# A filter beside expert layers: one filter part per slot, a fourth slot per unit, and the first transform moved into the plain stage

## Chip, core and metric

The kernel runs on one core of a Trainium2 chip. The metric is the device time of one execution in microseconds (us); lower is better.

## What is computed

The input `x` has 2048 tokens of 512 numbers. It is normalized (`xn`), and the output is a sum of three terms:

```python
xn = _layernorm(x, axis=-1)
return x + _A_ref(xn, A_w_r, A_w_i) + _B_ref(xn, B_wg, B_w1, B_w2)
```

`_A_ref` is a spectral filter: a two-dimensional real Fourier transform, a product with complex weights, and the inverse transform. `_B_ref` is a mixture of experts in which all 8 experts take part (K = 8 of E = 8), so that it is eight dense two-layer networks, each weighted by a gate per token:

```python
h = _gelu(jnp.einsum("nd,edf->nef", xt, w1))
y = jnp.einsum("nef,efd->ned", h, w2)
out = jnp.einsum("ne,ned->nd", cw, y)
```

Each expert has a hidden width of 1792. Every matmul operand is split into a high and a low part (fp32r), and a product is made of three passes over them.

## The kernel before

The hidden width is cut into chunks of 256, 56 in all over the experts. The first four (`N1 = 4`) are worked in the *plain stage*, two at a time in two passes `q`. A pass goes over four groups `t` of 512 tokens: four first-layer products (`mm1`: `s` for the chunk, `f` for its half, 12 matmuls each), then four second-layer products (`mm2`, 12 matmuls each), whose results VectorE adds to `acc` with the gate as factor. In `mm1` ScalarE applies the gelu and casts the result to the high part of `h`; the low part is a subtraction, on VectorE for `f == 0` and on GpSimd (POOL) for `f == 1`. Weights come into a buffer `raw` and are split by `part1` (first layer) and `part2` (second layer): cast on ScalarE, subtraction on POOL.

After each `mm1` and `mm2` group `tick()` lets a generator, `background()`, issue a bit of other work: normalization of the remaining tokens, logits and gates, the sums and differences of x (`sums`) that the later stage needs and their stores to DRAM (`xs`), and copies of tables (`copies`, one `next(copy)` each). Parts yield a cost; `PACE` is the credit per tick, and `NEXT` ends a tick. In the plain stage the scheduler of the language orders the instructions, with edges where `issue_after` asks for them. There are 64 ticks.

The other 52 chunks are taken in pairs, `N2 = 26`, and each pair in two *units* (`i`), 52 units `u`. A unit multiplies 2x2 blocks by seven products instead of eight (a Strassen-Winograd scheme): `layer1` makes seven products of 12 matmuls from x (`xin` loads `b11`, `b21`, `T1` to `T4`, `b22` into three buffers `xr`) with prepared weights, and `layer2`, interleaved with it, makes the seven products of the unit before and adds each into `acc` (`into`, VectorE). The products go to three PSUM tiles `A`, `B`, `C` of two banks; `layer2` puts two products into one tile one after the other, so the second may not start before the first has been added to `acc`. Weights of the next pair are loaded into the single buffer `raw` and split (`prepare`, ScalarE and POOL). Here the order on each engine is pinned to that of the program (`pin`); DMAs are not pinned.

The filter is worked twice (`filtered(0)`, `filtered(1)`: even and odd frequencies), each as 100 parts `(pe, dve, cost)`: a load of tables, 19 parts of the forward transform (with matmuls), 60 parts without matmuls (butterflies `radix4`, `twiddle`, `multiply` and `combine`), another load, and 19 parts of the inverse transform (with matmuls). Every instruction of them is recorded at line 390 (`op`), every DMA at line 179 (`move`). All wait in the queue `chunks`. A unit has three slots for them, in the steps `n` = 0, 2 and 3 of its seven. In `slot_pe` a slot takes one part with matmuls, or parts without as long as their costs add up to at most 3.2; `slot_dve` issues their VectorE and ScalarE work:

```python
while chunks and not (todo and (chunks[0][0] or spent + chunks[0][2] > 3.2)):
    pe, dve, cost = taken()
```

In `dve` of the forward transform the order is: cast and low part of the product `px` (tile X), copy of the product `py` to `Y`, cast and low part of `u`, two more ScalarE operations on X, then the sum or difference of the halves of the next input `us` (`sgn_op`), then the loads of the next `us` (`part`) and the next table (`table`).

In the first unit there is no second layer to interleave, and `X` and `Z` are both made by matmuls with `a11`; in every other unit ScalarE copies `X` to `Z`.

Of the kernel before, what the change touches and what calls it, by code (L numbers as in the profile page):

```python
# [95 lines left out]
def body(ctx: ExitStack, tc: tile.TileContext, io):  # L96
# [282 lines left out]
    def filtered(p):  # L379
# [38 lines left out]
        for k in range(NB + 3):  # L418
# [10 lines left out]
            def dve(k=k):  # L429
                X = None  # L430
                if 0 <= k - 2 < NB:
                    X = quarters("BC"[k % 2])[:, :, :, :R2].rearrange("p i h (c r) -> p i h c r", c=2)
                    of["X", k - 2] = X
                    px = of["px"].rearrange("p (c r) -> p c r", c=2)
                    op(A.copy, X[:, 0, 0], px)
                    low(X[:, 0], px)
# [9 lines left out]
                if X is not None:  # L446
                    op(A.mul, X[:, 1, :, 0], r32(X[:, 0, :, 1]), -1.0)
                    op(A.copy, X[:, 1, :, 1], r32(X[:, 0, :, 0]))
                if k < NB:
                    u1 = of["us", k]  # L450
                    op(V.tensor_tensor, u1[:, :2], u1[:, :2], u1[:, 2:], op=sgn_op)
                if k + 1 < NB:
# [183 lines left out]
    def mm1(w1, t, s, f):  # L636
# [8 lines left out]
        h = hp.tile([P, 2, TB], F32R, name="h")  # L645
        if f == 0:
            nc.scalar.activation(p1, p1, AF.Gelu_apprx_tanh)
            last_dve[0] = split(h, p1)
        else:
            c = hp.tile([P, TB], F32, name="c", bufs=1)  # L650
            nc.scalar.activation(c, p1, AF.Gelu_apprx_tanh)
            for cs in (slice(0, P), slice(P, TB)) if s else (slice(0, TB),):
                last_pool[0] = split(h[:, :, cs], c[:, cs], nc.gpsimd)
# [81 lines left out]
    def background():  # L735

        n4, n8, s8, s0, s1, sp = ln_rest(4, 4), ln_rest(8, 8), ln_stats(8, 8), sums(0), sums(1), spread()
        for part in (
# [7 lines left out]
            gates((1,)), islice(n8, 1), gap(),  # L746
            islice(n8, 2), gap(), islice(n8, 2), gap(),
            islice(n8, 1), islice(s0, 1), gap(),
            islice(n8, 1), gap(),
            islice(n8, 1), islice(s0, 1), gap(),  # L750
            n8, gap(),
            logits_a((2, 3)), gap(), logits_b((2, 3)), gap(), gates((2, 3)), gap(),
            islice(s0, 1), gap(), islice(s0, 1), gap(), s0, gap(),
# [4 lines left out]
        for cost in s1:  # L758
            next(stores, None)
            yield cost  # L760
            yield NEXT
        for _ in stores:
            yield NEXT
        for _ in range(6):
            next(copy)
            yield NEXT
            yield NEXT

    chunks = deque(filtered(0) + filtered(1))
    todo = []  # L770
# [7 lines left out]
    def slot_pe():  # L778

        spent = 0.0  # L780
        while chunks and not (todo and (chunks[0][0] or spent + chunks[0][2] > 3.2)):
            pe, dve, cost = taken()
            spent += 3.2 if pe else cost
            if pe:
                pe()
            todo.append(dve)
# [6 lines left out]
    bg, step1 = background(), iter(())  # L793
    busy, credit, handed = True, 5.0, False

# [6 lines left out]
    def tick():  # L802
# [4 lines left out]
        while delayed and delayed[0][0] <= 0:  # L807
            delayed.pop(0)[1]()
        if handed:
            with tc.issue_after(last_pool[0]), tc.issue_after(last_act[0]):  # L810
                next(step1, None)
# [73 lines left out]

    ahead = {}

# [3 lines left out]
    def xin(n, i):  # L891
        if (n, i) in ahead:
            return ahead.pop((n, i))
        x = xr.tile([P, 2, 2, TB], F32R, name="xr", bufs=3)
        nc.sync.dma_start(r32(x), xs[n][i])
        return x
# [25 lines left out]
    def layer1(c, i, w, hs, old):  # L922
# [14 lines left out]
        product(X, w["a11"], x, True)  # L937
        Z = bank("A")
        if first:
            product(Z, w["a11"], x, True)  # L940
            ahead["T3", i] = xin("T3", i)
            nc.sync.dma_start(raw, io["wb"][0])
        else:
            copy_of(Z, X)
        yield
# [36 lines left out]

        if first:
            B = bank("B")
            product(B, w["s3"], xin("T3", i), True)
        product(Z, w["s1"], xin("T1", i), False)
# [140 lines left out]
    for q in range(N1 // 2):  # L1127
        more = 2 * q + 2 < N1
        for t in range(NT):
            h = ahead_h  # L1130
            for s in range(2):
                for f in range(len(h) if s == 0 else 0, NFT):
                    h.append(mm1(w1[s], t, s, f))
                    if q == 0 and t == 0 and s == 0:
                        with tc.issue_after(last_act[0]):
                            w2.append(part2(f))
                        delay(4, lambda f=f: load_part(2 + f, 0, f))
                if t == 0 and s == 0 and q:
                    w2.append(part2(1))
                    if more:  # L1140
# [15 lines left out]
            if not more and t + 2 == NT:  # L1156
                for _ in bg:
                    pass
                busy, handed = False, True
                early.close()  # L1160
# [3 lines left out]
                xr = ctx.enter_context(tc.tile_pool(name="xr", bufs=1, reuse_waits="tile"))  # L1164
                ahead = {(n, 0): xin(n, 0) for n in ("b11", "b21", "T2")}
        if more:
            w2 = [part2(0)]
    for b in range(NB - 4, NB):
# [9 lines left out]
    for u in range(2 * N2):  # L1178
# [4 lines left out]
        if u == 1:  # L1183
            ahead.update({(n, 1): xin(n, 1) for n in ("b11", "b21", "T2")})
        if i == 1 and c + 1 < N2:
            raw = load(io["wa"][c + 1])
            step1 = prepare(wq, "u", sums1(raw, False), w1q)
# [23 lines left out]
        for n in range(7):  # L1211
            next(one)
            if u and n in (0, 2) and not end:
                slot_pe()
# [70 lines left out]
```

## Time and profile before

| What | Value |
|---|---|
| Median of 3 runs | 2441.81 us (2431.17 to 2442.25) |
| Profiled execution: time, span | 2437.74 us, 2436.0 us |
| TensorE busy | 2346.9 us (96%) |
| VectorE (DVE) busy | 1841.7 us (76%) |
| ScalarE (ACT) busy | 1105.3 us (45%) |
| GpSimd (POOL) busy | 1350.2 us (55%) |
| Mean granted TensorE clock | 0.989 |

Each number of the trace below comes from this one profiled execution. PE is TensorE's matmuls, PEld its weight loads, SP the engine that issues most DMAs. "L390" is line 390 of the kernel. A group's row has the line, the engine, the operation, the tiles it writes and reads, shapes and a count, then the busy time in us and the mean of one in ns. In the order of time a row begins with start and duration, and a bracket tells how long the engine sat idle before it and what ended that. A row of a stretch `A:B` has its length, then per engine the busy time and the number of instructions, the granted clock (1.00 is full), the share of the DMA engines, and GB/s.

The plain stage runs to 225.42 us, where the first matmul of line 880 (the units' products) starts; the units fill the rest.

### The profile page before, as it was taken

To read this page: it belongs to the slowest core of one execution; us is meant where nothing else is said; L and a number is where in the kernel's file an instruction comes from. 1 tells how busy PE (TensorE), PEld (TensorE's weight loads), DVE (VectorE), ACT (ScalarE), POOL (GpSimd) and SP (SyncE) were. 2 spreads that over 40 slices of the span, in tenths; PEclk is the share of its full clock that TensorE was granted. 3 is DMA by queue.
4 is the path that set the end of the run, shared out by engine and by line. 5 is a ranking of instruction groups with operands and counts; after the bars stand their busy time and mean duration, and the time that the engine had idled before them with its cause. 6 is when DMAs were issued, how large, how long until landed. Compare 5 with 4: busy or idle time off the path is not lost.

```text
span 2436.0 us, 28116 instructions
## 1 busy us (share of the span) xinstructions
PE 2346.9 (96%) x10640; PEld 1921.4 (79%) x10640; DVE 1841.7 (76%) x1729; ACT 1105.3 (45%) x1549; POOL 1350.2 (55%) x788
## 2 busy tenths in 40 slices
PE   9998899999988989999999999999999999999999
PEld 7776788887766777888888888777777888888888
DVE  7511577779999999777777777899989777777776
ACT  6422464554433444444445554444444444444441
POOL 2215455565654666555555555765666555566663
PEclk9999999999999999999999999999999999999999
DMA  4772777665655657787766766666656778886663
GB/s 175 268 286 88 257 267 277 245 256 216 234 215 216 220 204 275 268 285 269 255 243 249 249 242 237 216 221 219 229 202 222 284 260 286 286 287 222 238 223 115
DMA packets 130152, 579.13 MB, mean 238 GB/s; under 512 B 13761, under 2 KB 24513, under 8 KB 75105
## 3 DMA queue, kind: packets, MB, share of 16 engines
q1 hardware_dynamic: 129360, 564.65, 64.4%
q10 hardware_dynamic: 656, 12.67, 1.3%
q8 instruction: 85, 1.39, 0.2%
q14 instruction: 51, 0.41, 0.1%
HBM read 541.49 MB, written 48.37 MB: 242 GB/s over the span
## 4 chain that ended last, share of the span: by engine, by line
PE 74%; DVE 19%; issue 3%; DMA 2%; POOL 2%; ACT 1%; SPq 0%; DVEq 0%; POOLq 0%; ACTq 0%
PE B L880 28%; PE C L880 19%; PE A L880 17%; DVE Y L390 5%; PE psf L390 4%; DVE acc L909 3%; DVE c L912 3%; DVE c L932 3%; PE p L642 2%; PE p L667 2%; DVE hs L919 1%; DVE B L390 1%; DVE A L390 1%; DMA raw<-in_wp 1%; DVE c L909 1%
## 5 line engine op out<-in xcount | busy, mean ns | idle before, releaser
L919 POOL TENSOR_TENSOR hs<-c,hs 128x1024 fp32r<-128x1024 f32 x155 | 409.2, 2640 | 404.0 <-ACT hs L916 399.6
L880 PE MATMUL C<-hs,vs 128*128 128x512 f32 x1836 | 452.1, 395 | 16.1 <-DVE acc L909 14.9
L916 ACT CAST hs<-c 128x1024 fp32r<-128x1024 f32 x361 | 379.2, 1051 | 178.2 <-PE B L880 91.7
L880 PE MATMUL B<-xr,ua 128*128 128x512 f32 x1872 | 455.2, 392 | 2.4 <-DVE c L909 1.3
L880 PE MATMUL A<-xr,us 128*128 128x512 f32 x1872 | 454.8, 392 | 1.2 <-issue 1.2
L880 PEld LDWEIGHTS C<-hs,vs 128*128 128x128 f32 x1836 | 345.6, 190 | 95.7 <-DVE acc L909 18.3
L880 PEld LDWEIGHTS B<-xr,ua 128*128 128x128 f32 x1872 | 351.4, 188 | 82.0 <-DVE c L909 3.1
L880 PEld LDWEIGHTS A<-xr,us 128*128 128x128 f32 x1872 | 349.7, 188 | 77.5 <-issue 1.6
L880 PE MATMUL B<-hs,va 128*128 128x512 f32 x1224 | 302.6, 396 | 17.8 <-DVE acc L909 17.8
L912 DVE TENSOR_TENSOR c<-c 128x1024 f32<-128x1024 f32 x204 | 309.1, 1515 | 0.1
L919 DVE TENSOR_TENSOR hs<-c,hs 128x1024 fp32r<-128x1024 f32 x206 | 297.1, 1462 | 1.2 <-ACT hs L916 1.2
L880 PEld LDWEIGHTS B<-hs,va 128*128 128x128 f32 x1224 | 228.9, 189 | 74.0 <-DVE acc L909 24.9
L909 DVE TENSOR_TENSOR acc<-C,acc 128x1024 f32<-128x1024 f32 x198 | 241.3, 1219 | 59.4 <-PE C L880 58.5
L903 ACT ACTIVATE c<-c 128x1024 f32<-128x1024 f32 x104 | 110.4, 1062 | 280.4 <-DVE c L909 280.4
L899 ACT COPY c<-A 128x1024 f32<-128x1024 f32 x104 | 105.6, 1015 | 258.9 <-PE A L880 147.8
L932 DVE TENSOR_TENSOR c<-c,cwb 128x1024 f32<-128x1024 f32 x104 | 162.2, 1560 | 57.5 <-ACT c L903 57.5
L909 DVE TENSOR_TENSOR acc<-B,acc 128x1024 f32<-128x1024 f32 x100 | 122.1, 1221 | 86.8 <-PE B L880 86.7
L621 POOL TENSOR_TENSOR ua<-raw,ua 128x512 fp32r<-128x512 f32 x78 | 118.0, 1513 | 119.7 <-ACT ua L620 119.7
L880 PE MATMUL C<-hs,va 128*128 128x512 f32 x612 | 156.0, 405 | 24.0 <-DVE acc L909 24.0
L909 DVE TENSOR_TENSOR c<-B,c 128x1024 f32<-128x1024 f32 x104 | 127.0, 1222 | 53.1 <-PE B L880 34.2
L880 PE MATMUL B<-xr,us 128*128 128x512 f32 x624 | 152.9, 394 | 10.1 <-DMA xr<-xs_T 10.1
L880 PEld LDWEIGHTS C<-hs,va 128*128 128x128 f32 x612 | 117.2, 194 | 56.3 <-DVE acc L909 30.6
(184 smaller groups left out, 3137.0 us busy)
## 6 DMA issues: line engine op xcount, KB each, us to landing
xr<-xs_T SPq DMA_DIRECT2D x208, 1024.0 KB, 5.7
xr<-xs_b SPq DMA_DIRECT2D x156, 1024.0 KB, 5.3
cwb<-cwd SPq DMA_DIRECT2D x120, 256.0 KB, 5.5
raw<-in_wa SPq DMA_DIRECT2D x26, 1024.0 KB, 4.9
raw<-in_wb SPq DMA_DIRECT2D x26, 1024.0 KB, 4.8
xs_T<-Y SPq DMA_DIRECT2D x8, 1024.0 KB, 6.5
us<-xfd SPq DMA_DIRECT2D x32, 256.0 KB, 3.1
D<-mbd SPq DMA_DIRECT2D x32, 256.0 KB, 3.9
```

The costliest lines, as they stand in the source:

```text
L390: return pin(fn(*args, **kw))
L621: return pin((eng or nc.vector).tensor_tensor(dst[:, 1], src, r32(dst[:, 0]), op=ALU.subtract)).ins
L642: last = nc.tensor.matmul(p1, w1[k][:, hw, f * P : (f + 1) * P], x, start=(n == 0), stop=(n == 11))
L667: last = nc.tensor.matmul(p2, h[f][:, hh, js], w2[f][:, hw], start=(n == 0), stop=(n == 6 * NFT - 1))
L880: pin(nc.tensor.matmul(pt[:, m, :], w[:, hw, k, m * P : (m + 1) * P], x[:, hx, k, :], start=(start and n == 0), stop=(n == 5), skip_group_ ...
L899: last_act[0] = pin(nc.scalar.copy(dst, src)).ins
L903: last_act[0] = pin(nc.scalar.activation(v, v, AF.Gelu_apprx_tanh)).ins
L909: pin(nc.vector.tensor_add(dst, a, b))
L912: pin(nc.vector.tensor_sub(dst, a, b))
L916: main_act[0] = pin(nc.scalar.copy(hs[n][:, 0], src)).ins
L919: op = (nc.gpsimd if pool else nc.vector).tensor_tensor(hs[n][:, 1], src, r32(hs[n][:, 0]), op=ALU.subtract)
L932: pin(nc.vector.tensor_mul(dst, src, g))
```

## The change

- A slot takes exactly one filter part. A fourth slot is opened in step `n == 5` where the next part has matmuls or a cost under 1.3. The three short table loads that follow other parts are merged into the part ahead of them.
- The first 20 parts (the first filter's load and forward transform) are issued by `background()` in the plain stage, one per tick, in place of six copies; five copies move to earlier ticks and the rest are taken in the units.
- `handed` has three values now: the plain stage's last group drains the background only until the x sums are stored, and from then on all h splits are VectorE's.
- In the forward transform the sum or difference of the halves of `us` comes first in `dve`.
- In the second plain pass the second-layer weights are split behind the first `mm1` groups, not ahead of them.
- In the first unit `Z` is copied from `X` as elsewhere; the product with `T3` comes second, into `C`; `b11`, `T3`, `b21` are loaded ahead, and the load of the next first-layer weights is issued behind the second unit's `b11`.

```diff
             def dve(k=k):
                 X = None
+                if k < NB:
+                    u1 = of["us", k]
+                    op(V.tensor_tensor, u1[:, :2], u1[:, :2], u1[:, 2:], op=sgn_op)
...
-                if k < NB:
-                    u1 = of["us", k]
-                    op(V.tensor_tensor, u1[:, :2], u1[:, :2], u1[:, 2:], op=sgn_op)
...
-        if f == 0:
+        if f == 0 or handed > 0:
             nc.scalar.activation(p1, p1, AF.Gelu_apprx_tanh)
             last_dve[0] = split(h, p1)
...
         for _ in stores:
+            part_of_filter()
             yield NEXT
-        for _ in range(6):
-            next(copy)
+        handed = 0
+        while len(chunks) > 177:
+            part_of_filter()
             yield NEXT
-            yield NEXT
-
-    chunks = deque(filtered(0) + filtered(1))
+
+    chunks = deque()
+    for pe, dve, cost in filtered(0) + filtered(1):
+        if chunks and cost < 0.5:
+            ahead_pe, ahead_dve, ahead_cost = chunks.pop()
+            chunks.append((ahead_pe, lambda a=ahead_dve, b=dve: (a(), b()), ahead_cost))
+        else:
+            chunks.append((pe, dve, cost))
+
+    def part_of_filter():
+
+        pe, dve, cost = chunks.popleft()
+        if pe:
+            pe()
+        dve()
...
     def slot_pe():
 
-        spent = 0.0
-        while chunks and not (todo and (chunks[0][0] or spent + chunks[0][2] > 3.2)):
+        if chunks:
             pe, dve, cost = taken()
-            spent += 3.2 if pe else cost
             if pe:
                 pe()
             todo.append(dve)
...
         Z = bank("A")
+        copy_of(Z, X)
         if first:
-            product(Z, w["a11"], x, True)
-            ahead["T3", i] = xin("T3", i)
+            B = bank("C")
+            product(B, w["s3"], xin("T3", i), True)
             nc.sync.dma_start(raw, io["wb"][0])
-        else:
-            copy_of(Z, X)
...
-        if first:
-            B = bank("B")
-            product(B, w["s3"], xin("T3", i), True)
         product(Z, w["s1"], xin("T1", i), False)
...
                     h.append(mm1(w1[s], t, s, f))
+                    if q and t == 0 and s == 1 and f == 0:
+                        w2.append(part2(1))
...
                 if t == 0 and s == 0 and q:
-                    w2.append(part2(1))
+                    w2.append(part2(0))
...
             if not more and t + 2 == NT:
-                for _ in bg:
-                    pass
-                busy, handed = False, True
+                while handed < 0:
+                    next(bg)
+                handed = 1
...
-                ahead = {(n, 0): xin(n, 0) for n in ("b11", "b21", "T2")}
+                ahead = {(n, 0): xin(n, 0) for n in ("b11", "T3", "b21")}
         if more:
-            w2 = [part2(0)]
+            w2 = []
...
         if u == 1:
-            ahead.update({(n, 1): xin(n, 1) for n in ("b11", "b21", "T2")})
+            ahead.update({(n, 1): xin(n, 1) for n in ("b11",)})
+            behind = last_x[0]
+            ahead.update({(n, 1): xin(n, 1) for n in ("b21", "T2")})
         if i == 1 and c + 1 < N2:
-            raw = load(io["wa"][c + 1])
+            with tc.issue_after(behind) if u == 1 else nullcontext():
+                raw = load(io["wa"][c + 1])
...
-            if u and n in (0, 2) and not end:
+            if u and not end and (n in (0, 2) or n == 5 and chunks and (chunks[0][0] or chunks[0][2] < 1.3)):
                 slot_pe()
```

More of the change, by code (lines that the diff above doesn't have):

```diff
@@ L735, in background @@
     def background():
+        nonlocal handed
         n4, n8, s8, s0, s1, sp = ln_rest(4, 4), ln_rest(8, 8), ln_stats(8, 8), sums(0), sums(1), spread()
@@ L746, in background @@
             gates((1,)), islice(n8, 1), gap(),
-            islice(n8, 2), gap(), islice(n8, 2), gap(),
+            islice(n8, 2), gap(), islice(n8, 2), copied(), gap(),
             islice(n8, 1), islice(s0, 1), gap(),
-            islice(n8, 1), gap(),
+            islice(n8, 1), copied(), gap(),
             islice(n8, 1), islice(s0, 1), gap(),
-            n8, gap(),
-            logits_a((2, 3)), gap(), logits_b((2, 3)), gap(), gates((2, 3)), gap(),
+            n8, copied(), gap(),
+            logits_a((2, 3)), gap(), logits_b((2, 3)), copied(), gap(), gates((2, 3)), copied(), gap(),
             islice(s0, 1), gap(), islice(s0, 1), gap(), s0, gap(),
@@ L793, in body @@
     bg, step1 = background(), iter(())
-    busy, credit, handed = True, 5.0, False
+    busy, credit, handed = True, 5.0, -1
     delayed = []
@@ L808, in tick @@
             delayed.pop(0)[1]()
-        if handed:
+        if handed > 0:
             with tc.issue_after(last_pool[0]), tc.issue_after(last_act[0]):
@@ L884, in product @@
                     n += 1
-    ahead = {}
+    ahead, last_x = {}, [None]
     def bank(name):
@@ L894, in xin @@
         x = xr.tile([P, 2, 2, TB], F32R, name="xr", bufs=3)
-        nc.sync.dma_start(r32(x), xs[n][i])
+        last_x[0] = nc.sync.dma_start(r32(x), xs[n][i]).ins
         return x
```

## The prediction

> **What bounds the kernel now.** The page comes first: TensorE (PE) is busy for nearly the whole span, so only its gaps, and work it does twice, are worth time. The waits of PE, summed by releaser, say what its gaps are.
>
> ```profile
> span 2436.0 us, 28116 instructions
> PE 2346.9 (96%) x10640; PEld 1921.4 (79%) x10640; DVE 1841.7 (76%) x1729; ACT 1105.3 (45%) x1549; POOL 1350.2 (55%) x788
> PE C L880 <- DVE acc L909: 38.9, 21, 4.2
> PE B L880 <- DVE acc L909: 17.8, 16, 3.7
> PE B L880 <- DMA xr<-xs_T: 10.1, 1, 10.1
> PE p L642 <- ACT c L651: 5.6, 1, 5.6
> PE p L667 <- POOL h L621: 4.2, 2, 3.0
> ```
>
> Read as: line of the waiting matmul, what released it, total, times, longest. 56.7 us go to matmuls of the second layer that may not write a PSUM bank until VectorE (DVE) has added the last product in it to `acc`. The other three waits are single events near the start.
>
> The waits on DVE lie in two stretches. The next rows give PE's busy time and matmul count there for line 880 alone, for all engines (PE, PEld, DVE, ACT, POOL; granted clock; DMA), and for the filter's line 390 alone; the third stretch has no filter work.
>
> ```profile
> 555.00:945.00 390.00, 355.69 (x1491) 284.01 (x1490) 0.97 0.60 220
> 1490.00:1905.00 415.00, 391.86 (x1664) 313.52 (x1663) 0.99 0.63 224
> 2160.00:2360.00 200.00, 200.00 (x874) 163.61 (x873) 1.00 0.65 233
> ...
> 555.00:945.00 390.00, 355.69 (x1491) 284.01 (x1490) 367.13 (x307) 165.32 (x221) 233.19 (x125) 0.97 0.60 220
> ...
> 555.00:945.00 390.00, 0.00 (x0) 0.00 (x0) 130.87 (x120) 7.90 (x36) 0.97 0.60 220
> 1490.00:1905.00 415.00, 0.88 (x6) 0.86 (x6) 113.13 (x93) 9.17 (x39) 0.99 0.63 224
> ```
>
> Calm matmuls take 200.00/874 = 0.2288 us, so a unit of 168 takes 38.4 us. At that rate the first stretch's 1491 need 341.2 us and the second's 1664 need 380.8 (and 0.9 of the filter's): lost are 48.8 and 33.3, together **82.1 us**. That is more than the waits, because the clock drops after some. These stretches are the filter's steps without matmuls (butterflies, twiddles, multiplication by the weights), two or three in each of three slots per unit. DVE is 94% busy in the first: it is the bound there. Take from the filter's DVE time what a unit absorbs free of loss: (130.87 - 48.8)/8.875 units = 9.25 us in the first, (113.13 - 33.3)/9.9 = 8.06 in the second, 8.6 over both.
>
> **The change, part by part.**
>
> *One part per slot, a fourth slot.* I laid the 177 remaining parts on the 50 units by the new rule (three slots, a fourth where the next part has matmuls or is estimated under 1.3); they end in unit 50. What matters is the DVE time per unit.
>
> ```profile
> 690.00:804.00 114.00, 0.00 (x0) 0.00 (x0) 44.51 (x64) 0.00 (x0) 0.96 0.61 226
> 1638.00:1742.00 104.00, 0.00 (x0) 0.00 (x0) 34.92 (x32) 0.00 (x0) 0.98 0.63 225
> L390 DVE TENSOR_TENSOR Y<-Y 128x1024 f32<-128x1024 f32 x24 | 50.0, 2082 | 0.6
> L390 DVE TENSOR_TENSOR Y<-A,B 128x512 f32<-128x512 f32 x24 | 32.6, 1415 | 0.0
> L390 DVE TENSOR_TENSOR Y<-A,B 128x520 f32<-128x520 f32 x8 | 13.9, 1793 | 0.0
> ```
>
> The first two rows are line 390 while the eight multiply-and-combine pairs run: 5.56 us a pair in the first filter, 4.37 in the second. A butterfly part is one operation of 2.1 us, or at its end two of 32.6/24 = 1.36 (first filter 13.9/8 = 1.74). A butterfly unit then holds 6 to 7 us, under 8.6: no loss. A unit of four multiply parts holds two pairs: 11.1 in the first filter (three units, 2.5 over each), and 6.95 + 5.56 = 12.5 in the unit that two heavy butterfly steps open (3.9 over); in the second, 8.7 three times (0.1 over) and 5.4 + 4.4 = 9.8 once (1.2 over). Remaining loss 13 us; with 9.25 absorbed 9.5, with 8.06 18. Gain: 82.1 - 13 = **69** (64 to 72.6).
>
> By the Trainium skill ("TensorE: Matmul & The Clock Gate", Part 1: the HAM clock gate) the clock is halved only after an idle window of about 3.4 us, so remaining waits of 1 to 3 us would cost no clock. Scaling the 13 by 56.7/82.1 gives 9, and the sum would be 4 lower. I keep the row: 0.97 in a stretch whose longest wait was 4.2.
>
> *First unit.* A second product of `a11` with `b11` becomes a copy by ScalarE, `T3` is fetched ahead instead of `T2`, and the load of the next weights goes behind an x load.
>
> ```profile
> 228.28 2.88 PE L880 MATMUL A<-xr,ua 128*128 128x512 f32 x12
> 231.00 2.88 PE L880 MATMUL B<-xr,ua 128*128 128x512 f32 x12
> 246.74 4.34 PE L880 MATMUL B<-xr,us 128*128 128x512 f32 x12 [10.15 <-DMA xr<-xs_T]
> ...
> 239.24 0.33 SPq L127 DMA_DIRECT2D raw<-in_wa  x1
> 239.67 0.85 SPq L895 DMA_DIRECT2D xr<-xs_T  x2
> ...
> xr<-xs_T SPq DMA_DIRECT2D x208, 1024.0 KB, 5.7
> L899 ACT COPY A<-B 128x1024 f32<-128x1024 f32 x51 | 50.9, 997 | 78.8 <-PE B L880 45.2 <-DVE acc L909 33.6
> ```
>
> The duplicate costs 231.00 - 228.28 = 2.7. The wait of 10.15, with 4.34 - 2.88 = 1.5 of slow clock behind it, exists because SP stood at the weights' load until their buffer was read out (239.24), and the x loads came behind it. All three go: 14.3. Late next are the x loads themselves: three buffers, each free when its product ends, two products (5.5 us) ahead of use, against 5.7 to land and 0.3 to issue; four loads at up to 0.6 put back 2 (0 to 6 if they land 1 us later). The copy of 1.0 lies beside the next two products, and its result is needed after them. The weights' load, some 10 us later, serves unit 2. Net **12.3**.
>
> *Plain stage, stalls.* Second-layer weight casts move behind the gelus, and the last group's h splits go to DVE.
>
> ```profile
> 135.05 1.14 ACT L620 CAST w<-raw 128x512 fp32r<-128x512 f32 x2 [16.81 <-DMA raw<-in_wp]
> 135.75 2.50 POOL L621 TENSOR_TENSOR w<-raw,w 128x512 fp32r<-128x512 f32 x2 [15.72 <-ACT w L620]
> 137.24 7.30 PE L642 MATMUL p<-x,w 128*128 128x512 f32 x24 [5.58 <-ACT c L651]
> 212.70 11.87 PE L667 MATMUL p<-w,h 128*128 128x512 f32 x38 [3.04 <-POOL h L621]
> ```
>
> ScalarE stood 16.81 us at the cast for a late DMA with the gelus behind it: 5.58, and 7.30 - 24 x 0.2288 = 1.8 of slow clock. POOL's h split stood behind the layer weights: 3.04, and 11.87 - 38 x 0.2288 = 3.2. Both go: **13.6**. The casts are late next; from the second one until its product stand one matmul group and half of the next, 4.1 us, against two casts of 0.6 and two POOL subtractions of 1.3: nothing, if the DMA is in. The six queued copies of tables move from 110-170 us to some 48-80 us (the sixth later), where the DMA has room (0.41, below); their price is nothing as long as the x sums there are not on PE's path.
>
> *The first forward transform in the plain stage.* Its PE work (192 matmuls) only moves. New is the pace: one part in each group of 12 matmuls, 12 x 0.2288 + 2 x 0.72 = 4.2 us (0.72 from the next rows: 305.61 - 304.89). In units 2 to 7 a part had 10 us or more. With the sign step first on DVE and two `us` buffers, a part's load starts only after the low part of the one before: 3.1 to land, 0.3 to issue, three DVE steps of 0.42 make 4.7.
>
> ```profile
> 304.89 0.88 PE L390 MATMUL psf<-A,uz 128*128 128x260 f32 x6
> 305.61 0.62 PE L880 MATMUL C<-hs,vs 128*128 128x512 f32 x2
> us<-xfd SPq DMA_DIRECT2D x32, 256.0 KB, 3.1
> L390 DVE TENSOR_TENSOR uz<-us,uz x16: 409/425/1418, 287.2 to 500.0; 128x256 fp32r<-128x256 f32 x16
> ...
> 40.00:80.00 40.00, 39.67 (x194) 30.09 (x193) 25.09 (x65) 20.61 (x35) 2.71 (x3) 1.00 0.41 132
> 120.00:160.00 40.00, 34.42 (x144) 27.64 (x143) 7.47 (x10) 7.99 (x16) 7.74 (x8) 0.91 1.01 399
> 160.00:200.00 40.00, 40.00 (x178) 33.03 (x177) 8.98 (x13) 8.85 (x17) 5.44 (x6) 1.00 0.23 84
> ...
> q10 hardware_dynamic: 192, 5.25, 22.3%
> A<-f0d SPq DMA_DIRECT2D x1, 520.0 KB, 21.0
> 137.24 10.20 SPq L179 DMA_DIRECT2D us<-xfd  x2
> ```
>
> 16 parts x (4.7 - 4.2) put back **8** (0 to the bounds below). By the Trainium skill ("DMA: Bandwidth & Descriptors", Anatomy of one DMA, measured on another queue kind) 256 KB would take 2.0 + 0.6 us, the loop would keep pace and the sum would be 8 lower; the landing of 3.1 decides. The parts start at some 112 us, by my count of the ticks, in a DMA that is full until about 160 (1.01) with loads landing in up to 21.0. The copies that leave were 5.25 of that part's traffic (22.3%), but the filter's loads come in. Behind a waiting load stands DVE, and behind it the evictions of PE's banks. One first landing of 21 against three banks' room (8.2 us) and the two parts before the first matmul (8.4): 4, twice over for table and input: **8**. Queued on SP behind these loads are the next raw weights, needed 50 us later, and stores. DVE and ScalarE have room (7 to 9 of 40 us).
>
> Sum, against the profiled execution's 2437.74 us (span 2436.0 and 1.7 around it; 4.1 under the shown median 2441.81): 2437.7 - 69 - 12.3 - 13.6 + 8 + 8 = **2359**.
>
> **The rivals.** *A, the transform is paced by a full DMA.* If its first six parts wait as the second `us` load did (10.2 us behind the first, row above), they cost 6 x (10.2 - 4.2) = 36 instead of 8: 2387. For it: 1.01 at 120-160 us; against: 0.23 right after, and the copies gone.
>
> *B, the fourth slot hurts locally.* It puts a part ahead of the sixth and the next unit's first step, where DVE has most of its own work.
>
> ```profile
> 695.98 3.02 PE L880 MATMUL C<-hs,vs 128*128 128x512 f32 x12 [1.39 <-DVE acc L909]
> ```
>
> There a part at the first slot already made the eviction late by 1.39. 29 units have four parts; at 1.3 each: 2359 + 38 = 2397. Against: 8.6 us absorbed per unit, and matmul parts lengthen PE's own work.
>
> *C, slower.* If every one of the 16 steps in the plain stage waits for a landing of L, each costs L + 1.6 - 4.2. The other terms gain 95, so this decides from L = 8.5 us; at 10 us throughout it costs 118, and the time is 2461. For it: landings of 10 to 21 in the full stretch; against: the median of 3.1, and that most steps fall after 140 us.
>
> *D, nothing gained,* if the waits on DVE return in full inside units: its total work stays. Against: over the span DVE is busy 76%.
>
> **How the numbers follow.** Chances: forecast 0.66, A 0.12, B 0.12, C 0.06, D or mixtures near no change 0.04. The forecast's own range is 2337 (72.6 + 14.3 + 13.6 gained, nothing put back) to 2378. Up to B's 2397 the range leaves out C and D. Faster by over 0.5% 0.90, within 0.5% 0.04, slower 0.06; 0.5% (12 us) is about what a measurement of this kernel can tell from no change.
>
> **What would show it.** Right: waits of PE on `acc` fall from 56.7 to about 10, in the first filter's multiply units; the filter's line 390 shows matmuls from about 120 us; no PE wait on `xr` over 2 us; the waits on `c` and `h` in the plain stage gone. Wrong: PE waits at `psf` or on DVE between 110 and 190 us (A, C), or at `C` and `B` once per unit all along (B).

## The result, and the profile after

The changed kernel takes 2372.85 us (2369.38 to 2374.64, four runs) against 2441.72 before: a ratio of 0.9726 [0.9697, 0.9755]. The forecast was 2359, with a range of 2337 to 2397. The profiled execution took 2369.38, against 2437.74 before: 68.4 us less, where the sum of the terms had promised 79.

Two lines of the page after, and the waits of TensorE by releaser (line, what released it, total, times, longest). Line 880 is now 894, 909 is 923, 899 is 913.

```profile
span 2367.6 us, 28129 instructions
PE 2328.6 (98%) x10628; PEld 1909.1 (81%) x10628; DVE 1897.2 (80%) x1731; ACT 1107.9 (47%) x1549; POOL 1373.9 (58%) x785
```

```profile
PE C L894 <- DVE acc L923: 6.2, 4, 2.3
PE B L894 <- DVE c L923: 4.8, 6, 1.5
PE B L894 <- ACT A L913: 3.7, 1, 3.7
PE B L894 <- DVE acc L923: 3.5, 8, 0.8
PE A L894 <- issue: 2.4, 2, 1.2
```

The 56.7 us on `acc` have become 6.2 + 3.5 = 9.7, the wait on `xr` near the start is gone, and of those on `c` and `h` there 0.6 and 0.2 are left. VectorE is busy 55.5 us longer (1897.2 against 1841.7) for the same arithmetic and two h splits more.

The same parts now lie elsewhere, so the stretches differ: the first two rows hold the filter's steps without matmuls, the third the worst of them. Columns: length, PE and PEld busy time with counts of the products alone, granted clock, DMA share, GB/s.

```profile
320.00:980.00 660.00, 648.04 (x2802) 525.19 (x2801) 1.00 0.68 245
1380.00:2050.00 670.00, 667.15 (x2898) 542.82 (x2897) 1.00 0.66 236
530.00:700.00 170.00, 161.04 (x686) 128.55 (x685) 0.99 0.64 235
```

At 0.2288 us a matmul the first loses 660 - 641.1 - 0.9 (six filter matmuls) = 18.0, the second 670 - 663.1 = 6.9: **24.9** where 82.1 were lost before, so 57.2 gained. The forecast left 13. The 170 us around the first filter's multiplication lose 170 - 157.0 = 13.0 of it; the other 11.9 are scattered, 5.0 in the rest of the first stretch and 6.9 in the second.

The units start at 244.60 us (225.42 before). At start to start (0.72 for six) the 192 matmuls moved ahead of them are 23.0 us, so the plain stage lost 23.0 - 19.2 = 3.8 less than it did. The first unit, from its first product to the one behind the first two of the second layer, before and after, in order of time:

```profile
225.42 3.02 PE L880 MATMUL B<-xr,ua 128*128 128x512 f32 x12 [0.84 <-DVE acc L671]
...
269.10 2.92 PE L880 MATMUL B<-xr,ua 128*128 128x512 f32 x12
```

```profile
244.60 2.98 PE L894 MATMUL B<-xr,ua 128*128 128x512 f32 x12 [0.94 <-DVE acc L671]
...
282.18 2.91 PE L894 MATMUL B<-xr,ua 128*128 128x512 f32 x12
```

43.7 us became 37.6: 6.1 gained. Together 57.2 + 3.8 + 6.1 = 67.1 of the 68.4; 1.3 lie outside these places.

### The profile page after: what moved, and what is told of

The parts are those of the page before. It is cut to its first block, busy times and chain, and to the rows that moved or that the text cites. A ratio compares the mean times of both kernels' runs of the same rounds, so it can differ in the third digit from the quotient of the medians.

```text
span 2367.6 us, 28129 instructions
## 1 busy us (share of the span) xinstructions
PE 2328.6 (98%) x10628; PEld 1909.1 (81%) x10628; DVE 1897.2 (80%) x1731; ACT 1107.9 (47%) x1549; POOL 1373.9 (58%) x785
## 4 chain that ended last, share of the span: by engine, by line
PE 80%; DVE 14%; DMA 2%; ACT 1%; issue 1%; POOL 1%; SPq 0%; ACTq 0%; POOLq 0%; DVEq 0%
PE B L894 30%; PE C L894 20%; PE A L894 20%; PE psf L390 4%; PE p L642 3%; DVE Y L390 3%; PE p L667 2%; DVE c L946 2%; DVE acc L923 2%; DVE c L926 2%; DVE c L923 1%; DVE hs L933 1%; DVE B L390 1%; ACT c L917 1%; DVE A L390 1%
## 5 line engine op out<-in xcount | busy, mean ns | idle before, releaser
L933 POOL TENSOR_TENSOR hs<-c,hs 128x1024 fp32r<-128x1024 f32 x155 | 415.5, 2681 | 330.1 <-ACT hs L930 325.9
L933 DVE TENSOR_TENSOR hs<-c,hs 128x1024 fp32r<-128x1024 f32 x206 | 311.7, 1533 | 1.2 <-ACT hs L930 1.2
L926 DVE TENSOR_TENSOR c<-c 128x1024 f32<-128x1024 f32 x204 | 297.8, 1460 | 0.0
L923 DVE TENSOR_TENSOR acc<-C,acc 128x1024 f32<-128x1024 f32 x198 | 241.1, 1218 | 58.2 <-PE C L894 57.7
L894 PEld LDWEIGHTS B<-hs,va 128*128 128x128 f32 x1224 | 228.3, 188 | 56.7 <-DVE acc L923 6.9
L946 DVE TENSOR_TENSOR c<-c,cwb 128x1024 f32<-128x1024 f32 x104 | 177.9, 1711 | 57.5 <-ACT c L917 57.5
L621 POOL TENSOR_TENSOR ua<-raw,ua 128x512 fp32r<-128x512 f32 x78 | 132.4, 1697 | 143.6 <-ACT ua L620 143.6
L923 DVE TENSOR_TENSOR acc<-B,acc 128x1024 f32<-128x1024 f32 x100 | 122.1, 1221 | 61.5 <-PE B L894 61.1
L621 POOL TENSOR_TENSOR va<-raw,va 128x512 fp32r<-128x512 f32 x78 | 138.2, 1772 | 45.6 <-ACT va L620 44.2
L894 PE MATMUL C<-hs,va 128*128 128x512 f32 x612 | 149.6, 393 | 1.5 <-DVE acc L923 1.5
L894 PE MATMUL A<-hs,vs 128*128 128x512 f32 x612 | 148.6, 391 | 0.0
```

Source lines behind the costliest of these rows:

```text
L621: return pin((eng or nc.vector).tensor_tensor(dst[:, 1], src, r32(dst[:, 0]), op=ALU.subtract)).ins
L894: pin(nc.tensor.matmul(pt[:, m, :], w[:, hw, k, m * P : (m + 1) * P], x[:, hx, k, :], start=(start and n == 0), stop=(n == 5), skip_group_ ...
L923: pin(nc.vector.tensor_add(dst, a, b))
L926: pin(nc.vector.tensor_sub(dst, a, b))
L933: op = (nc.gpsimd if pool else nc.vector).tensor_tensor(hs[n][:, 1], src, r32(hs[n][:, 0]), op=ALU.subtract)
L946: pin(nc.vector.tensor_mul(dst, src, g))
```

## The experiments

Times are medians. Each set of kernels was timed beside its own runs of the kernel before, whose median was 2435.75 to 2441.72; ratios to it are given where a few us matter. The changed kernel itself ran again only beside two of them, the product and the sign step last; the others are compared with its 2372.85, and its own two medians differ by 3.5.

**The old slots.** Does the spreading bring the gain (theory S) or the move of the transform (theory M)?

```diff
-        if chunks:
+        spent = 0.0
+        while chunks and not (todo and (chunks[0][0] or spent + chunks[0][2] > 3.2)):
             pe, dve, cost = taken()
+            spent += 3.2 if pe else cost
...
-            if u and not end and (n in (0, 2) or n == 5 and chunks and (chunks[0][0] or chunks[0][2] < 1.3)):
+            if u and n in (0, 2) and not end:
```

> The changed kernel with the old slot rule: three slots per unit, parts without matmuls taken together up to an estimate of 3.2; the first forward transform stays in the plain stage. Theory S (spreading: a unit takes in some 8.6 us of filter work on VectorE, more makes TensorE wait): the two stretches without filter matmuls lose some 80 us again instead of 25, so 2373 + 57 = 2430 us, with 50 to 60 us of TensorE waits on acc. Rival M (the gain comes from the first transform's move, which leaves VectorE more room in all): the gain stays, 2373 to 2385 us.

2417.95, ratio 0.9918 [0.9892, 0.9945]; the waits on `acc` are back (line numbers differ by two):

```profile
PE C L896 <- DVE acc L925: 35.1, 17, 4.2
PE B L896 <- DVE acc L925: 11.2, 7, 2.5
```

S holds, 12 us under its 2430: spreading alone is worth 45 us. It isn't the whole 57 of the stretches. From the units' start to the end this kernel takes 2415.9 - 245.03 = 2170.9, the changed one 2123.0: 47.9 for spreading. The kernel before takes 2210.6, of which 23.0 are the moved matmuls and 6.1 the first unit, so 2181.5. By this subtraction the last 10.6 go with the 20 parts that no longer have to be placed in units; no run shows them by themselves.

**The transform back in the units**, with the fourth slot open to every part.

```diff
         for _ in stores:
-            part_of_filter()
             yield NEXT
         handed = 0
-        while len(chunks) > 177:
-            part_of_filter()
-            yield NEXT
...
-            if u and not end and (n in (0, 2) or n == 5 and chunks and (chunks[0][0] or chunks[0][2] < 1.3)):
+            if u and not end and n in (0, 2, 5):
```

> The changed kernel with the first forward transform back in the units, one part per slot, and the fourth slot open to every part (197 parts in 200 slots). Theory S: the 23 us of matmuls only go from the plain stage to the units, and the butterflies now stand four to a unit (8 to 9.5 us on VectorE, just over what a unit takes in), so the loss in the stretches grows from 25 to 35-50 us: 2383 to 2400 us. Rival M: without the move the gain is lost, 2425 us or more. Rival P (the move costs, because the plain stage waits for loads): 2365 us or less.

2387.30, ratio 0.9785 [0.976, 0.981], in theory S's range: the move is worth 14.5. The units start 25.4 us earlier (219.20), with 23.0 us of matmuls less ahead of them: beyond its own matmuls the transform costs the plain stage 2.4, where the forecast put back 16. From the units' start to the end this kernel needs 2384.2 - 219.20 = 2165.0, of which 23.0 are those matmuls: 19.0 more than the changed kernel. So the gain of the move is the room it leaves in the units (under a slot rule that differs in the fourth slot); there the waits rise:

```profile
PE C L890 <- DVE acc L919: 12.0, 6, 2.3
PE B L890 <- DVE c L919: 7.4, 9, 1.1
PE B L890 <- DVE acc L919: 6.0, 7, 1.1
```

**GpSimd without reads.** Left out of the computation here: the low parts of the units' weights and of their layer inputs that GpSimd makes; it writes zeros there instead. Theory L says that what still is lost comes from VectorE operations that last longer beside GpSimd's.

```diff
-                split(to[n], src.rearrange("p (k f) -> p k f", k=2), nc.gpsimd)
+                main_act[0] = pin(nc.scalar.copy(to[n][:, 0], src.rearrange("p (k f) -> p k f", k=2))).ins
+                pin(nc.gpsimd.memset(r32(to[n][:, 1]), 0.0))
...
-        op = (nc.gpsimd if pool else nc.vector).tensor_tensor(hs[n][:, 1], src, r32(hs[n][:, 0]), op=ALU.subtract)
+        op = nc.gpsimd.memset(r32(hs[n][:, 1]), 0.0) if pool else nc.vector.tensor_tensor(hs[n][:, 1], src, r32(hs[n][:, 0]), op=ALU.subtract)
```

> The changed kernel, in which GpSimd writes zeros in place of the low parts of the layer inputs and weights that it makes in the units (those low parts are left out of the computation); it reads no SBUF for them and is shorter. Theory L (a VectorE operation with two SBUF inputs is held up while GpSimd reads SBUF, and this makes the remaining loss of 25 us): VectorE's twiddle step falls from a median of 1.5 to 0.42 us, its 128x1024 operations to some 1.22, VectorE's busy time by 150 us or more, the loss to under 8: 2350 to 2358 us. Rival W (the parts are just too much work per unit, whatever GpSimd does): durations within 5% and 2368 to 2375 us.

2345.95, ratio 0.9613 [0.9584, 0.9642]. The same VectorE work takes 1642.3 us instead of 1897.2, and no wait on `acc` is left in the list. Groups of VectorE in the changed kernel, then here (count, busy time in us, mean in ns):

```profile
L390 DVE SCALAR_TENSOR_TENSOR Y<-Y,C 128x256 f32<-128x256 f32 x27 | 30.6, 1169 | 0.0
L390 DVE TENSOR_TENSOR us<-us 128x256 f32<-128x256 f32 x32 | 27.1, 848 | 10.0 <-DMA us<-xfd 10.0
```

```profile
L390 DVE SCALAR_TENSOR_TENSOR Y<-Y,C 128x256 f32<-128x256 f32 x27 | 10.3, 419 | 0.0
L390 DVE TENSOR_TENSOR us<-us 128x256 f32<-128x256 f32 x32 | 14.8, 463 | 12.5 <-DMA us<-xfd 12.5
320.00:980.00 660.00, 658.19 (x2869) 538.19 (x2868) 1.00 0.70 252
1380.00:2050.00 670.00, 670.00 (x2922) 548.23 (x2921) 1.00 0.67 239
```

The two stretches lose 660 - 656.4 - 18 x 0.12 (filter matmuls) = 1.4, and 670 - 668.6 = 1.4: of the 24.9 some 22 are gone. Theory L holds. The total passes its range by 4: from the units' start at 252.83 to the end it is 28.5 us less in all, and 5.5 of that are the first unit (284.87 - 252.83 = 32.0 instead of 37.6), whose copy no longer waits.

GpSimd's work is shorter here too (693.3 us busy instead of 1373.9), and some of its reads remain, so the trace can tell reading from mere work. VectorE's `c<-c,cwb`, both inputs in SBUF, keeps its 1.23 us at 582.03, while GpSimd writes zeros from 582.45 to 582.98. `B<-Y,D` takes 1.79 us at 573.37, beside a GpSimd operation that reads `raw` from 572.89 to 574.61, and 0.69 at 591.73, beside no GpSimd instruction.

**The first unit's copy on VectorE.** In the changed kernel a wait that the forecast didn't have stands there: `X` to `Z`, ScalarE's copy. First PE, then ScalarE, in order of time:

```profile
247.42 2.88 PE L894 MATMUL C<-xr,us 128*128 128x512 f32 x12
253.99 4.59 PE L894 MATMUL B<-xr,ua 128*128 128x512 f32 x12 [3.69 <-ACT A L913]
...
250.85 0.62 ACT L620 CAST vs<-raw 128x512 fp32r<-128x512 f32 x1 [2.90 <-POOL raw L852]
...
252.94 1.00 ACT L913 COPY A<-B 128x1024 f32<-128x1024 f32 x1
```

The copy stands in ScalarE's queue behind four weight casts, the first of which waits 2.90 us for GpSimd.

```diff
-        copy_of(Z, X)
+        if first:
+            pin(nc.vector.tensor_copy(Z, X))
+        else:
+            copy_of(Z, X)
```

> The changed kernel with the first unit's copy of X to Z on VectorE instead of ScalarE. Theory Q (the copy stands behind weight casts in ScalarE's queue, which wait for GpSimd): TensorE's wait of 3.7 us there goes, and 1.7 of slow clock behind it: 2373 - 5 = 2368 us. Rival X (the first unit is paced by its x loads and PSUM copies anyway): the wait comes back one or two products later, 2371 to 2374 us.

2367.89, ratio 0.9708 [0.9687, 0.9729]. The wait on the copy is gone, a wait of 1.27 on `xr` is next, and from the units' start to the product used above the kernel needs 281.08 - 249.03 = 32.1 us instead of 37.6. Theory Q holds in the trace: 5.5 gained there. The medians show 2 to 5 of it; the profiled execution shows 1.6 (2367.75 against 2369.38), because its units start 4.4 us later.

**The product instead of the copy.** As before the change, but with the x loads and `T3`'s product in the new order.

```diff
-        copy_of(Z, X)
+        if first:
+            product(Z, w["a11"], x, True)
+        else:
+            copy_of(Z, X)
```

> The changed kernel with the first unit's second accumulator made by the product once more, as in the kernel before, instead of the copy from PSUM to PSUM; the x loads stay in their new order. Theory Q (the copy is late in ScalarE's queue, and the step itself is what cost the first unit its gain): the product costs 2.7, and the waits of 3.7 on the copy and of 1.2 and 1.15 on the accumulator's reading go: 2368 to 2371, 2 to 5 us less than the changed kernel beside it. Theory X (behind the copy stands the fetch of x, which would be late by as much): a wait on xr of 3 us or more takes its place, and the time is 2373 to 2380.

2369.38, ratio 0.9730 [0.9711, 0.9749], beside 2369.37 of the changed kernel. The time lies in theory Q's range, but not its 2 to 5 us less: the totals are the same. In the trace the stretch takes 284.59 - 248.97 = 35.6, 2.0 less, with a wait of only 0.92 on `xr`, so X falls; but the plain stage ended 4.4 later. So in the first unit of these two executions the copy on ScalarE costs 2 more than the product it replaced. The new order, of the loads and of `T3`'s product together, brought 43.7 - 35.6 = 8.1.

**A fifth slot.** If the first filter's multiply units are too full (S), they should be spread further.

```diff
-            if u and not end and (n in (0, 2) or n == 5 and chunks and (chunks[0][0] or chunks[0][2] < 1.3)):
+            if u and not end and (n in (0, 2) or n in (4, 5) and chunks and (chunks[0][0] or n == 5 and chunks[0][2] < 1.1)):
```

> The changed kernel with one more place per unit that may take a filter part with matmuls (after the unit's fifth vector operation), while a small part without matmuls may stand only at the last place. Theory S (what is left of the loss in the first filter's multiply units is the same cause as before: parts whose matmuls cover less than their vector work, now 8 parts of the two heavy units that stand too close): more spreading takes 6 to 10 us off the 24.8 us that the two stretches still lose, 2363 to 2367 against 2372.9. Theory L alone (vector operations that stand beside GpSimd's are the whole remainder, and spreading can't help them, only put more of them beside GpSimd): 2370 to 2376, with the wait of product on acc not smaller than 6.2 + 3.5 us.

2367.94, ratio 0.9711 [0.9685, 0.9737]. The 170 us of the multiplication, and the waits:

```profile
530.00:700.00 170.00, 166.03 (x720) 134.43 (x720) 1.00 0.70 253
```

```profile
PE B L894 <- DVE acc L923: 8.4, 11, 1.6
PE B L894 <- DVE c L923: 2.2, 4, 0.6
```

720 matmuls: 5.3 lost instead of 13.0. The same parts need not lie in the same 170 us here, but the two whole stretches agree: 2840 and 2900 matmuls, 10.2 + 6.5 = 16.7 lost instead of 24.9. The wait at `C` is gone from the list, that at `B` grew from 3.5 to 8.4. The 8.2 are in theory S's 6 to 10, and the 8.4 on `acc` are less than L alone allows (6.2 + 3.5). The total, between the two theories' ranges, shows 1 to 5 of them against the two medians of the changed kernel.

**The best of both**: the fifth slot and the copy on VectorE (both edits above).

> The changed kernel with the five places and the first unit's copy from PSUM to PSUM on VectorE. If the two act in different places they add: the copy gave 5.0 us (2367.9), the fifth place 6 to 10 by theory S, so 2358 to 2362; by theory L alone no better than 2366 to 2370.

2361.84 (2361.53 to 2364.26), ratio 0.9689 [0.9664, 0.9715]. It lies in the range forecast and under all nine runs of the changed kernel (2368.65 to 2374.64). From the units' start to the end the trace has 2359.8 - 246.10 = 2113.7, so 9.3 less than the changed kernel; the copy alone has 6.0 less, the fifth slot alone 4.7. The two nearly add, as acts in different places should.

**The old cast order** in the second plain pass.

```diff
-                    if q and t == 0 and s == 1 and f == 0:
-                        w2.append(part2(1))
...
-                    w2.append(part2(0))
+                    w2.append(part2(1))
...
-            w2 = []
+            w2 = [part2(0)]
```

> The changed kernel with the plain stage's weight casts in the order that the kernel before had. Theory P (the reordering is what took the waits on c and h of 5.58 + 1.8 us out of the plain stage): 2378 to 2381, with a wait of the first groups' or the plain stage's matmuls on ScalarE of 4 to 7 us. Theory F (the first transform's matmuls, which now stand in the plain stage, fill those waits whatever the order is): 2371 to 2375, and no such wait over 2 us.

2371.42, ratio 0.9725 [0.9694, 0.9756], and the wait on `c` is 0.6 us in all. The time is F's. But the edit doesn't bring the old order back: in the plain stage the scheduler orders the instructions, and ScalarE, VectorE and GpSimd have the same sequence of rows in this trace as in the changed kernel's. So neither theory is tested, and what the order is worth stays open. The rows of the weights' load and its cast, in order of time, of the kernel before, of this one and of the changed kernel:

```profile
118.67 5.86 SPq L135 DMA_DIRECT2D raw<-in_wp  x2
```

```profile
136.84 1.20 SPq L135 DMA_DIRECT2D raw<-in_wp  x1
149.77 0.62 ACT L620 CAST w<-raw 128x512 fp32r<-128x512 f32 x1
```

```profile
136.64 1.18 SPq L135 DMA_DIRECT2D raw<-in_wp  x1
149.56 0.62 ACT L620 CAST w<-raw 128x512 fp32r<-128x512 f32 x1
```

In the last two the load is issued 18 us later and the cast doesn't wait at all, where ScalarE stood 16.81 us before. Whether that comes from the copies that left this stretch or from the groups that now stand ahead wasn't tried apart.

**The last h splits on GpSimd again.**

```diff
-        if f == 0 or handed > 0:
+        if f == 0:
```

> The changed kernel with the last plain group's splits of h on GpSimd again, as in the kernel before, not on the engines that the change chose. If they set the plain stage's end (theory H): the wait of 3.04 + 3.2 us at the last groups returns, 2376 to 2379, and the units start 3 to 6 us later after the last plain group's matmuls. If the other work of the stage covers them (theory F): 2371 to 2375.

2377.60, ratio 0.9745 [0.9717, 0.9773]. The wait of 3.04 of the kernel before returns:

```profile
242.11 8.91 PE L667 MATMUL p<-w,h 128*128 128x512 f32 x38 [3.03 <-POOL h L621]
```

The slow clock behind it doesn't: 38 matmuls take 8.91 us, and took 11.87 before. So this edit is worth 3, not 6.2 (4.8 by the medians; the runs overlap). The units of this execution start 7.3 later, at 251.86, but 2.6 of that stand before the filter's first matmul (152.79 against 150.22), ahead of the edit.

**The changed kernel once more, and the sign step last.**

> The changed kernel once more, unaltered, beside the next two. 2369 to 2376 us. What it is to tell is how far the end of the plain stage moves from execution to execution of the same instructions: kernels whose plain stage is the same as here started their units at 244.6, 246.1, 248.5, 249.0 and 252.8 us. Theory V (it is no property of the kernels but varies by run): a start of the units other than 244.6, by 1 to 8 us, with the same instructions. Theory K (each kernel has its own): 244.6 within 0.5.

> The changed kernel with the forward transform's sign step after the other vector steps of its part, as in the kernel before, not ahead of them. Theory N (its place is nothing, since a part's load has time enough): within 2 us of the changed kernel beside it. Theory P (in the plain stage a part's load is the pace, and the sign step first lengthens the way from one landing to the next load, as my prediction had it with 0.5 us a part): 4 to 8 us less than the changed kernel beside it, the units starting that much earlier.

```diff
-                if k < NB:
-                    u1 = of["us", k]
-                    op(V.tensor_tensor, u1[:, :2], u1[:, :2], u1[:, 2:], op=sgn_op)
                 if 0 <= k - 2 < NB:
...
                     op(A.mul, X[:, 1, :, 0], r32(X[:, 0, :, 1]), -1.0)
                     op(A.copy, X[:, 1, :, 1], r32(X[:, 0, :, 0]))
+                if k < NB:
+                    u1 = of["us", k]
+                    op(V.tensor_tensor, u1[:, :2], u1[:, :2], u1[:, 2:], op=sgn_op)
```

The repeat took 2369.37 (2368.65 to 2371.66), ratio 0.9735 [0.9718, 0.9752], with the units' start at 244.64: by its letter theory K. But the starts listed there go with the granted clock that the same execution had from 80 to 100 us, in work that all these kernels share: 1.00 where the units start at 244.6 and 246.1, 0.91 at 248.5, 0.83 at 249.0 and 252.8. The runs of one kernel differ by 6 us (2364.93 to 2371.44 with the product), and only the profiled one shows its start, so K isn't settled.

The sign step last gave 2372.43, ratio 0.9745 [0.9728, 0.9762]: 3 us more, with the units' start 2.4 later. That is no price of the step: the filter's first matmul already starts 2.6 later (152.81 against 150.22), and from the units' start to the end this kernel needs 1.1 less. In the plain stage the edit hardly acts. There the scheduler orders VectorE's instructions, and the 48 of the transform stand in the same order in both traces, but for one sign step that changes places with the low part beside it. So P's 4 to 8 us less didn't come, N's 2 us are passed by 1, and neither is tested.

## Why the prediction held, and where its terms were off

**Spreading: -69, measured -57.2.** The mechanism is the one forecast, and so is the place of the largest rest: 11.4 us were left to the first filter's multiply units, and 13.0 are lost in the stretch that holds them. The step that failed is "a butterfly unit then holds 6 to 7 us, under 8.6: no loss". Some 12 us are lost in small pieces outside the first filter's multiply units, where that sum left 1.5. (Redone, the sum leaves 17.2 with 8.06 absorbed, not 18, and the bounds given with the terms, 64 gained here and 6 put back in the first unit, bring the forecast's upper end to 2368, not 2378.) The count of VectorE time per unit was taken from rows of before, but the same operations last longer or shorter by what GpSimd does at that moment. VectorE and GpSimd in the changed kernel, in order of time:

```profile
597.40 0.70 DVE L390 TENSOR_TENSOR A<-Y,D 128x520 f32<-128x520 f32 x1
598.02 2.88 DVE L390 TENSOR_TENSOR B<-Y,D 128x520 f32<-128x520 f32 x1
600.82 1.21 DVE L923 TENSOR_TENSOR acc<-C,acc 128x1024 f32<-128x1024 f32 x1
...
597.58 2.75 POOL L933 TENSOR_TENSOR hs<-c,hs 128x1024 fp32r<-128x1024 f32 x1 [1.38 <-ACT hs L930]
...
602.08 4.61 PE L894 MATMUL C<-hs,vs 128*128 128x512 f32 x12 [2.34 <-DVE acc L923]
```

Two equal operations take 0.70 and 2.88 us; the second lasts until just after GpSimd's has ended at 600.33. The eviction behind it is late by that, and PE waits 2.34. The twelve matmuls behind the wait take 4.61, where the next twelve take 2.91: the granted clock is 0.58 and 0.56 from 602 to 606 us. So here a wait under 3 us did cost clock, as the sum had kept it. The third experiment removes GpSimd's reads for the low parts, and the waits on `acc` with them. By the Trainium skill ("SBUF — State Buffer", Who interferes with whom) a VectorE instruction with two SBUF inputs contends with a GpSimd instruction that reads SBUF, and not with one that only writes it. The trace agrees: the group `acc<-C,acc`, one input in PSUM, has a mean of 1218 ns in the changed kernel and 1221 in the third experiment, and the Y<-Y,C group falls from 1169 to 419 ns where GpSimd writes zeros instead.

**First unit: -12.3, measured -6.1.** The duplicate product and the 10.1 us wait on `xr` went as forecast. The failed step is "the copy of 1.0 lies beside the next two products, and its result is needed after them": one product stands between, since the next product into the copied-from tile comes after `T3`'s alone, and ScalarE had casts ahead of it. That is the 3.69, with 4.59 - 2.88 = 1.7 of slow clock behind it. `T3`'s product had also stood between two products into the second accumulator and covered one of its readings; before, the trace has one wait of 1.20 at `A`, and after it 2.4 in two. The 2 us put back for late x loads were not seen; with the copy on VectorE, 1.27 of them appear.

**Plain stage: -13.6 and +16, measured -3.8.** Both sums were too large. Of the stalls, the h splits were worth 3 by their experiment (their wait before was two events of 4.2 in all, not a single one). The 5.58 on the gelus went down to 0.6; no run shows that the order of the casts did it. Longer in the stage is a wait of the gate's logits (0.3 before), which the forecast doesn't have, and new are short waits of the transform:

```profile
PE psf L285 <- DVE x L263: 1.9, 1, 1.9
PE psf L390 <- issue: 1.5, 1, 1.5
PE psf L390 <- DMA D<-mbd: 0.9, 2, 0.7
PE psf L390 <- DVE uz L390: 0.9, 2, 0.6
```

The transform's own waits are 3.3 and not 16 (in the other executions the one on `D` alone was 0.7 to 5.6). Its 16 sign steps start from 144.8 to 197.2 us, 52.4/15 = 3.5 apart, so the chain of 4.7 from landing to next load wasn't the pace. The loads didn't land sooner than the 3.1 of the sum: the median is 4.5 (2.5 to 8.9). What failed is "With the sign step first on DVE": the scheduler put low parts of the part before ahead of sign steps, so that two loads are under way at a time. The load issued at 156.71 is used at 162.29, and the next is issued at 159.32. And the first load was issued at 131.5 and not at 112, the first matmul started at 150 and not at about 120, behind nine groups of the first layer that were put ahead:

```profile
123.37 25.31 PE L642 MATMUL p<-x,w 128*128 128x512 f32 x108
150.22 0.95 PE L390 MATMUL psf<-A,uz 128*128 128x260 f32 x6 [1.53 <-issue]
```

Rivals A and C fell on that: the first six sign steps lie 3.8 apart, not 10.2, and the median landing of 4.5 is far from C's 8.5 throughout, though the DMA was still 0.66 to 0.95 busy from 150 to 190 us. Rival B's wait exists, but the waits on DVE at `B` and `C` are 18 with 14.5 us in all (list of waits above), not 38 in 29 units, and one slot more made the kernel faster. Rival D fell with the result: 9.7 of the 56.7 us on `acc` are left.

The errors: 12 and 6 us too much gain in the units, 6 too little in the plain stage: 12 in all, and 10.5 with the 1.3 found outside these places. That the plain stage took some of the error back is luck, two errors that nearly cancel: the stalls gave some 7 us (3.8 + 3.3) instead of 13.6, and the transform's waits took 3.3 instead of 16.

## What to carry to other kernels

Here it paid to lay a queue of side work one small piece per gap, and to judge the gaps by what the busiest unit holds, not by the total; where a unit was still too full, another slot helped a little more. The durations of VectorE operations with two SBUF inputs are no constants while GpSimd reads: a budget from one placement carries to another only within that uncertainty, and taking such reads out of the way may be worth more than the next reordering. Where a scheduler orders the instructions, look in the trace whether an edit changed their order before reading its time. When a matmul is replaced by a copy on another engine, look at what stands in that engine's queue ahead of it, and at what the matmul had been covering.

## What the runs showed of the hardware beside that

The granted clock fell to half behind short waits in one execution and not in another, at the same place in the same work. Windows of the stretch from 80 to 86 us, of the changed kernel, then of the one with the sign step last (columns: PE busy, clock, DMA share, GB/s):

```profile
80.00:82.00 2.00, 0.25 (x2) 1.00 1.47 492
82.00:84.00 2.00, 2.00 (x12) 1.00 0.08 33
84.00:86.00 2.00, 1.10 (x9) 1.00 0.45 124
```

```profile
80.00:82.00 2.00, 0.13 (x1) 1.00 0.40 131
82.00:84.00 2.00, 1.96 (x6) 0.69 1.14 393
84.00:86.00 2.00, 1.87 (x10) 0.50 0.38 97
```

The longest wait there is 1.91 us in both. In the ten microseconds from 80 us the changed kernel executed 36 matmuls, the one with the copy on VectorE, whose instructions up to there are the same, 26:

```profile
80.00:90.00 10.00, 7.35 (x36) 1.00 0.81 236
```

```profile
80.00:90.00 10.00, 7.57 (x26) 0.66 0.79 261
```

Ten matmuls are 2.3 us of the 4.4 by which its units started later. Other executions show the same: in five whose clock was 1.00 from 80 to 100 us (the changed kernel, its repeat, the old slots, the best of both, the old cast order) the filter's first matmul starts at 150.2 to 150.7 us, in four at 0.83 (GpSimd without reads, the copy on VectorE, the last h splits, the sign step last) at 152.8 to 153.1. It isn't the only place: the product instead of the copy had 1.00 there, and its first filter matmul starts at 153.99. By the Trainium skill ("TensorE: Matmul & The Clock Gate", Part 1: The HAM clock gate) the gate looks at free-running windows of about 3.4 us, so that the same work can fall on either side. That would fit the two executions; that it takes an idle window of that length isn't what the row shows, where the longest wait is 1.91. What decides which of the two an execution gets wasn't tried.
